# First group of four turned by TensorE, second feature block and output copies at its joint moved, third slot tile behind the gate sums

## The chip, the cores and the metric

One Trainium2 chip, one core of it. The metric is the time of the whole program on the device in microseconds, the median of several runs; a profile is one further execution.

## The reference, cut to what matters

Three parts follow each other on 2304 tokens of 512 features, all in float32.

```python
scores = q @ k^T / 8                       # 4 x 8 heads, 576 positions, 64 wide
x = (scores * gamma**(i-j), i >= j) @ v    # retention, then tokens x 512
logits = x @ w_gate + log1p(exp(x @ w_noise)) * noise
x = sum over the top 2 of 8 experts: w * (relu(x @ w1[e]) @ w2[e])
h = x @ w_in                               # 512 -> 2048
out = (h * clip(h + 3, 0, 6) / 6) @ w_out  # 2048 -> 512
```

## The kernel before, in words

The order of the work on each engine is the order in which the Python code emits it; nothing is rescheduled. Every engine (TensorE is PE, VectorE DVE, ScalarE ACT, GpSimd POOL, SyncE SP) takes its instructions in order, and a DMA issue stands in the order of the engine whose queue it uses. Buffers come from pools: a tile of a pool that is in use makes its first writer wait.

**Attention** runs over 18 token tiles of 128 (`attention`). After every third tile `gsum` and `gate` compute the logits of the gate for the group and append a generator `route`, which picks two experts a token and computes the slots of the token's rows in a DRAM tensor `xe`. Each `rstep()` advances the first generator by one `yield`; so `rstep()` calls, scattered over the program, set where routing stands between the other work. The matmuls at L332 to L335 count the tokens (ranks) from the picks `ra`. `send` scatters one row block into `xe` (L374), an indirect DMA of POOL.

**Experts** (`moe`) run in ten sweeps (`SW`), each over the slots of one expert or a part of them. A sweep reads its tokens from `xe`, turns them so that features lie on partitions, and does a first GEMM (L688, into `ga` or `gb`) and a second (L705) for 8 feature blocks; the second GEMM of a block is emitted by `flush` one block later. Expert 0's three tiles of 120 slots are turned by PE in the last turn of `attention` (`x_tile`, L655 to L658). Results go to a DRAM tensor `yd`.

**The last layer** (`moe2`) takes the tokens in groups `GR`: two tiles in `plain`, then four groups of four in `seven`. For each tile `x2_gather` fetches the two experts' rows of each token from `yd` (L830), `x2_mix` weights and adds them (L838 on ACT, L839 on DVE). Then the tile must be turned. DVE turns blocks of 32x32 only, so the mixed tile is written to `x2d` in DRAM (L859) and read back by four DMAs that place each block of 32 tokens (`x_blocks`, L633), after which one DVE transposition finishes it (L874). The first group of four is prepared while `plain` runs its 16 steps f, in `x2_prep(1, f - 1)`; the table `PLAN` says in which step s = f - 1 each tile is gathered, mixed, read back and turned. The reads of this group are issued on ACT's queue, those of later groups on POOL's.

`seven` computes the four products of a 2x2 block matrix with seven multiplications (`g1_seven`): sums of the weights lie ready in the DRAM tensor `wc`, and sums of the tokens are built by `x2_sums`; `x2_set` splits each of the seven token operands into a high and a low float32r part (L908, L909). A block p of the 8 has seven sets of six matmuls (L1072), whose intermediate sums ACT copies out of PSUM (`mc`, L1077), then the hidden layer of both halves c[0] and c[1] (`hidden`, L1103 to L1107), then by `flush` the second GEMM of the block before. The last `flush` of a group copies the finished output tiles out of PSUM (L1130) and writes them (L1132). `wc_load` loads the weights of a block; a tiny DMA `paced` that reads an ACT result (L981) holds SP's queue until the program has come that far.

```python
                self.ys[j] = self.x_blocks(rows, (self.nc.sync, self.nc.scalar, self.nc.gpsimd)[min(gi, 2)])
            ((0, 4, 6, 8), (0, 5, 7, 9), (1, 6, 8, 10), (4, 7, 9, 11)),
```

The second line is the group's row of `PLAN`: for each of its four tiles the step s of gather, mix, read back and turn.

Of the kernel before, what the change touches and what calls it, by code (L numbers as in the profile page):

```python
# [7 lines left out]
F32 = mybir.dt.float32  # L8
# [56 lines left out]
class K:  # L65
# [210 lines left out]
    def route(self, g0, G):  # L276
# [51 lines left out]
        yield  # L328
        o = 128 + g0 // 3 % 2 * 32
# [71 lines left out]
    def attention(self):  # L401
# [25 lines left out]
        for t in range(NT):  # L427
# [19 lines left out]
            if t + 1 == NT:  # L447
                xs = self.x_new(0)
                for j, tag in enumerate(("acc", "gb", "tp")):
                    self.x_tile(0, xs, j, tag)  # L450
# [20 lines left out]
        self.gsum(NT // 3 - 1)  # L471
        self.xt(NT - 1)
# [338 lines left out]
    def flush(self):  # L811
# [4 lines left out]
        if self.prev[-1][4]:  # L816
            self.fin[0](*self.fin[1:])
# [18 lines left out]
    def x2_mix(self, t, y):  # L836
        v = self.nc.vector
        self.nc.scalar.activation(y[0], y[0], AF.Copy, scale=self.gw[:, t, 0:1])  # L838
        v.scalar_tensor_tensor(y[0], y[1], self.gw[:, t, 1:2], y[0], op0=OP.mult, op1=OP.add)  # L839

    def x2_prep(self, gi, s):
# [11 lines left out]
        for j in range(G):  # L853
# [3 lines left out]
            if s == plan[j][1]:  # L857
                self.x2_mix(t0 + j, self.ys[j])
                self.nc.gpsimd.dma_start(rows, self.ys[j][0])  # L859
        for j in range(G):  # L860
            rows = self.x2d[(t0 + j) * P:(t0 + j + 1) * P]
            _, _, get, cut = plan[j]
            if s == get:
                self.ys[j] = self.x_blocks(rows, (self.nc.sync, self.nc.scalar, self.nc.gpsimd)[min(gi, 2)])
            if s == cut:
# [4 lines left out]
                else:  # L870
                    if j % 2 == 0:
                        self.raw2.append(self.big([P, 4, 2 * P]))
                    o = self.raw2[-1][:, :, c]
                    self.nc.vector.transpose(o.rearrange("p b (t j) -> p t b j", j=32),  # L874
                                             x.rearrange("p t (b i) -> p t b i", i=32))
        if gi and s == 10:
# [3 lines left out]
            self.x2_set(*((1, 2) if gi == 1 else (1,)))  # L880
        if gi and s == 12:
            self.x2_sums()
        if gi == 1 and s == 13:
            self.x2_set(5, 3)

    def x2_sums(self):
# [4 lines left out]
        t2, t3, t4 = (self.row([P, DM]) for _ in range(3))  # L891
        v.tensor_sub(t3, b22, b12)
        v.tensor_sub(b12, b12, b11)
        v.tensor_sub(t2, b22, b12)
        v.tensor_sub(t4, t2, b21)
        self.x2f.update({3: b22, 4: t4, 5: b12, 6: t2, 7: t3})

    PLAN = (((0, 2, 4, 5), (0, 2, 4, 5)),
            ((0, 4, 6, 8), (0, 5, 7, 9), (1, 6, 8, 10), (4, 7, 9, 11)),
# [12 lines left out]
    def pr_init(self):  # L912
# [4 lines left out]
        self.wcn, self.wcs, self.late = 0, {}, None  # L917
# [87 lines left out]
    def plain(self, t0, G):  # L1005

        for f in range(16):
# [7 lines left out]
            if fi == 0:  # L1015
                self.wc_load(p + 2 if p < 6 else p + 1, gh.bitcast(F32))
            if f == 15:
                self.x2_set(6, 4, 7)
# [8 lines left out]
    def seven(self, gi, t0, G):  # L1027

        X = self.x2s
        for p in range(8):  # L1030
# [7 lines left out]
            joint = p == 7 and gi + 1 < len(self.GR)  # L1038
# [3 lines left out]
            else:  # L1042
                h.append(self.hidden(c[1]))
            self.flush()
# [10 lines left out]
            if joint:  # L1055
# [6 lines left out]
    def g1_seven(self, X, W, begun):  # L1062
# [33 lines left out]
        v.tensor_add(h1[:, n:], a, c5)  # L1096
        return h0, h1
# [239 lines left out]
```

## Time and profile before

| | us |
|---|---|
| median of 3 runs | 966.65 (965.6 to 969.04) |
| the profiled execution | 966.33 |
| its span, first to last instruction | 964.5 |
| PE busy | 939.6 (97%) |
| DVE, ACT, POOL busy | 614.5, 471.5, 239.6 |
| mean granted clock | 0.993 |

PE is the engine that is nearly always busy. Its time falls into attention (to about 112 us), the ten expert sweeps (to about 563), `plain` (to about 616) and the four groups of `seven`. The end of a matmul is modelled and matmuls overlap, so from one start to the next is what a set costs.

### The profile page before, as it was taken

Reading aid. Unit: us, or ns where it says so; the run is one execution under the profiler, and the core shown is the slowest. Engines: PE = TensorE matmul, PEld = TensorE weight load, DVE = VectorE, ACT = ScalarE, POOL = GpSimd, SP = SyncE. Lnnn points to the kernel's source line nnn. Section 1 sums busy time; section 2 is a strip of 40 time slices with the busy share of each in tenths; the row PEclk is TensorE's granted clock in tenths of the full one; section 3 lists DMA queues with packets and bytes.
Section 4 is the critical chain, followed back from the end, with each engine's and each line's share of the span. In section 5 each row is a group of like instructions: output and inputs, shape, how many; then the busy total and the mean of one; then the engine's idle time right before and its main releaser. Section 6 shows DMA issues by size and latency. Waiting matters only on the chain.

```text
span 964.5 us, 17639 instructions
## 1 busy us (share of the span) xinstructions
PE 939.6 (97%) x6248; PEld 835.5 (87%) x6248; DVE 614.5 (64%) x1356; ACT 471.5 (49%) x1000; POOL 239.6 (25%) x327
## 2 busy tenths in 40 slices
PE   8999999999999999999999997899999999999997
PEld 6888788888898988888888886788899899989986
DVE  5688664877879888786866444645654564564342
ACT  4566533546555464646444443444454454445442
POOL 1245332322425242332410213015013211500000
PEclk9999999999999999999999999999999999999999
DMA  9783746886969889797627788558667756965551
GB/s 341 266 309 134 268 144 203 269 239 202 294 224 274 257 253 279 224 260 265 204 104 238 238 284 301 205 198 291 206 241 260 254 186 228 296 197 196 195 189 47
DMA packets 126271, 223.30 MB, mean 232 GB/s; under 512 B 13269, under 2 KB 63189, under 8 KB 126173
## 3 DMA queue, kind: packets, MB, share of 16 engines
q1 hardware_dynamic: 113757, 190.47, 59.8%
q0 software_dynamic: 9680, 29.77, 9.1%
q10 hardware_dynamic: 2736, 1.84, 0.6%
q8 instruction: 51, 0.84, 0.4%
q14 instruction: 47, 0.39, 0.1%
HBM read 165.01 MB, written 57.02 MB: 230 GB/s over the span
## 4 chain that ended last, share of the span: by engine, by line
PE 87%; DVE 4%; DMA 4%; issue 2%; ACT 2%; ACTq 0%; POOL 0%; SPq 0%; DVEq 0%
PE p L705 39%; PE ga L688 12%; PE gb L688 9%; PE mga L1072 7%; PE p L1072 5%; PE mtp L1072 2%; PE mgb L1072 2%; PE px L214 2%; PE sc L192 2%; PE p L175 2%; PE px L204 2%; DMA b<-wc 1%; DMA s<-x2d 1%; PE p L253 1%; PE p L238 1%
## 5 line engine op out<-in xcount | busy, mean ns | idle before, releaser
L705 PE MATMUL p<-b,h 128*120 128x512 f32 (+1 forms) x1056 | 262.7, 396 | 5.3 <-ACT h L1117 5.2
L705 PEld LDWEIGHTS p<-b,h 128*120 128x120 f32 (+1 forms) x1056 | 189.3, 185 | 48.3 <-ACT h L1117 6.0
L705 PE MATMUL p<-b,b 128*128 128x512 f32 x768 | 180.0, 390 | 0.0
L705 PEld LDWEIGHTS p<-b,b 128*128 128x128 f32 x768 | 142.2, 188 | 28.2
L688 PE MATMUL ga<-x,b 128*128 128x360 f32 (+1 forms) x768 | 134.0, 323 | 1.8 <-DVE h L747 1.8
L688 PEld LDWEIGHTS ga<-x,b 128*128 128x128 f32 x768 | 124.7, 188 | 10.8 <-DVE h L747 6.2
L591 POOL TENSOR_TENSOR cvl<-cvl,cvs 128x256 f32<-128x256 f32 x64 | 50.2, 784 | 228.3 <-ACT cva L572 167.9
L542 DVE TENSOR_TENSOR b<-b,b 128x512 fp32r<-128x512 f32 x128 | 90.1, 738 | 13.4 <-ACT b L541 12.9
L688 PE MATMUL gb<-b,b 128*128 128x256 f32 x672 | 90.0, 283 | 0.3 <-DVE b L644 0.3
L688 PEld LDWEIGHTS gb<-b,b 128*128 128x128 f32 x672 | 87.1, 190 | 1.5 <-DVE b L644 0.5
L830 POOL DMA_INDIRECT s<-yd,slotc x36 | 37.7, 1047 | 167.3 <-DVE x L909 50.9
L541 ACT ACTIVATE b<-b 128x512 fp32r<-128x512 f32 x128 | 74.0, 625 | 0.0
L1107 DVE SCALAR_TENSOR_TENSOR b<-s,b 128x512 fp32r<-128x512 f32 x64 | 44.3, 692 | 44.7 <-ACT b L1106 43.3
L1106 ACT ACTIVATE b<-s 128x512 fp32r<-128x512 f32 x64 | 40.5, 632 | 53.7 <-DVE s L1104 52.8
L592 POOL TENSOR_TENSOR cvl<-cvt,cvl 128x256 f32<-128x256 f32 x64 | 58.9, 920 | 5.0
L1103 ACT ACTIVATE s<-s,three 128x512 f32<-128x512 f32 x64 | 45.9, 717 | 26.2 <-DVE s L1093 26.2
L1072 PE MATMUL mga<-b,b 128*128 128x256 f32 x384 | 56.6, 283 | 2.1 <-DMA b<-wc 2.1
L1093 DVE TENSOR_TENSOR s<-p,mc 128x256 f32<-128x256 f32 x32 | 13.6, 424 | 69.2 <-PE p L1072 69.2
L1072 PEld LDWEIGHTS mga<-b,b 128*128 128x128 f32 x384 | 52.6, 191 | 5.0 <-DMA b<-wc 2.6
L747 DVE SCALAR_TENSOR_TENSOR h<-gb,h 128x256 fp32r<-128x256 f32 (+1 forms) x64 | 27.6, 432 | 44.6 <-PE p L705 33.6
L1077 ACT ACTIVATE mc<-mga 128x256 f32<-128x256 f32 x64 | 24.5, 383 | 55.7 <-PE mga L1072 54.3
L747 DVE SCALAR_TENSOR_TENSOR h<-ga,h 128x360 fp32r<-128x360 f32 (+1 forms) x64 | 32.6, 510 | 24.6 <-ACT h L746 24.6
(190 smaller groups left out, 1451.6 us busy)
## 6 DMA issues: line engine op xcount, KB each, us to landing
b<-wc SPq DMA_DIRECT2D x112, 512.0 KB
b<-in_moe_w_dram SPq DMA_DIRECT2D x64, 512.0 KB
wc<-b SPq DMA_DIRECT2D x32, 512.0 KB
s<-xe SPq DMA_DIRECT2D x140, 64.0 KB
s<-in_moe_w_in_dram SPq DMA_DIRECT2D x32, 256.0 KB
s<-in_moe_w_out_dram SPq DMA_DIRECT2D x32, 256.0 KB
b<-wc SPq DMA_DIRECT2D x32, 256.0 KB
yd<-s SPq DMA_DIRECT2D x24, 240.0 KB
```

What stands on the lines that cost most here:

```text
L541: self.nc.scalar.activation(h, a, AF.Copy)
L542: rest = lambda h=h, l=l, a=a: self.nc.vector.tensor_sub(l, a, h.bitcast(F32))
L591: nc.gpsimd.tensor_mul(lf, lf, s.bitcast(F32))
L592: nc.gpsimd.tensor_add(lf, t.bitcast(F32), lf)
L688: nc.tensor.matmul(p, a[k], b[:, k, :n], start=(i == 0), stop=(i == 11))
L705: nc.tensor.matmul(a[:R], x[:, c], y[:, fi, :], start=(first and i == 0), stop=(last and i == 2))
L747: nc.vector.scalar_tensor_tensor(hl, p, 0.0, hh.bitcast(F32), op0=OP.max, op1=OP.subtract)
L830: nc.gpsimd.indirect_dma_start(out=r, out_offset=None, in_=self.yd[0:rows], in_offset=bass.IndirectOffsetOnAxis(ap=self.slotc[:, t, k:k + ...
L1072: nc.tensor.matmul(t, w[:, u, k], x[:, z, k], start=(first and i == 0), stop=(last and i == 5), skip_group_check=True)
L1103: nc.scalar.activation(r, x, AF.Relu, bias=self.three)
L1106: nc.scalar.activation(h[:, 0], x, AF.Copy, scale=1.0 / 6.0)
L1107: v.scalar_tensor_tensor(h[:, 1], x, 1.0 / 6.0, h[:, 0].bitcast(F32), op0=OP.mult, op1=OP.subtract)
```

## The change

For the first group of four only (gi == 1) `x2_mix` writes its result in another order of columns, in four pieces, into a new row tile; `x2_pe` turns it with four PE products against the identity into a PSUM tile, and ACT copies that out. The writes to `x2d`, the reads and the DVE transpositions of this group are gone. The steps of `PLAN` move, and so do the sums and splits. In `plain` the first weights of the next group are loaded at f = 12 (`min(p + 2, 8)`) instead of f = 14, and operand 7 is split a step earlier. In the first block of `seven` the second half of the hidden layer is put off into the next block (`late`, as at the other joints), and the two output copies of `plain` to the end of the next block's seven products (`late_out`). In attention the last gate group's rank matmuls come one `yield` later, and the third slot tile of expert 0 is turned after the last `gsum`.

```diff
--- before.py
+++ after.py
@@ -326,6 +326,8 @@
         yield
         yield
         yield
+        if g0 + G == NT:
+            yield
         o = 128 + g0 // 3 % 2 * 32
         pr = self.pg[:, o:o + G * 8].rearrange("p (g e) -> p g e", g=G)
         for g in range(G):
@@ -446,8 +448,8 @@
             self.kv(t)
             if t + 1 == NT:
                 xs = self.x_new(0)
-                for j, tag in enumerate(("acc", "gb", "tp")):
-                    self.x_tile(0, xs, j, tag)
+                self.x_tile(0, xs, 0, "acc")
+                self.x_tile(0, xs, 1, "gb")
             self.rstep()
             if t + 3 < NT:
                 self.ks(t + 3)
@@ -469,6 +471,7 @@
             if t + 1 < NT:
                 self.wstep(WN)
         self.gsum(NT // 3 - 1)
+        self.x_tile(0, xs, 2, "tp")
         self.xt(NT - 1)
         self.gate(NT - 1, groups)
         self.rstep()
@@ -808,13 +811,16 @@
             for s in sw:
                 xs.pop(s)
 
-    def flush(self):
+    def flush(self, out=True):
         if self.prev is None:
             return
         for g in self.prev:
             self.g2(*g)
         if self.prev[-1][4]:
-            self.fin[0](*self.fin[1:])
+            if out:
+                self.fin[0](*self.fin[1:])
+            else:
+                self.late_out = self.fin
         self.prev = None
 
 
@@ -833,10 +839,18 @@
             y.append(r)
         return y
 
-    def x2_mix(self, t, y):
+    def x2_mix(self, t, y, turned):
         v = self.nc.vector
         self.nc.scalar.activation(y[0], y[0], AF.Copy, scale=self.gw[:, t, 0:1])
-        v.scalar_tensor_tensor(y[0], y[1], self.gw[:, t, 1:2], y[0], op0=OP.mult, op1=OP.add)
+        if not turned:
+            v.scalar_tensor_tensor(y[0], y[1], self.gw[:, t, 1:2], y[0], op0=OP.mult, op1=OP.add)
+            return y[0]
+        z = self.row([P, DM])
+        o = z.rearrange("t (b q i) -> t b q i", q=4, b=4)
+        b, a = (u.rearrange("t (q b i) -> t q b i", q=4, b=4) for u in y)
+        for q in range(4):
+            v.scalar_tensor_tensor(o[:, :, q], a[:, q], self.gw[:, t, 1:2], b[:, q], op0=OP.mult, op1=OP.add)
+        return z
 
     def x2_prep(self, gi, s):
 
@@ -855,13 +869,14 @@
             if s == plan[j][0]:
                 self.ys[j] = self.x2_gather(t0 + j)
             if s == plan[j][1]:
-                self.x2_mix(t0 + j, self.ys[j])
-                self.nc.gpsimd.dma_start(rows, self.ys[j][0])
+                self.ys[j] = self.x2_mix(t0 + j, self.ys[j], gi == 1)
+                if gi != 1:
+                    self.nc.gpsimd.dma_start(rows, self.ys[j])
         for j in range(G):
             rows = self.x2d[(t0 + j) * P:(t0 + j + 1) * P]
             _, _, get, cut = plan[j]
-            if s == get:
-                self.ys[j] = self.x_blocks(rows, (self.nc.sync, self.nc.scalar, self.nc.gpsimd)[min(gi, 2)])
+            if s == get and gi != 1:
+                self.ys[j] = self.x_blocks(rows, self.nc.gpsimd if gi else None)
             if s == cut:
                 x = self.ys.pop(j)
                 c = slice(j % 2 * P, (j % 2 + 1) * P)
@@ -871,32 +886,50 @@
                     if j % 2 == 0:
                         self.raw2.append(self.big([P, 4, 2 * P]))
                     o = self.raw2[-1][:, :, c]
+                    if gi == 1:
+                        self.x2_pe(x, o)
+                        continue
                     self.nc.vector.transpose(o.rearrange("p b (t j) -> p t b j", j=32),
                                              x.rearrange("p t (b i) -> p t b i", i=32))
-        if gi and s == 10:
+        if gi and s == (8 if gi == 1 else 10):
             self.x2s = {}
             r = self.raw2[0].rearrange("p (h k) n -> p h (k n)", h=2)
             self.x2f = {1: r[:, 0], 2: r[:, 1]}
-            self.x2_set(*((1, 2) if gi == 1 else (1,)))
-        if gi and s == 12:
-            self.x2_sums()
-        if gi == 1 and s == 13:
-            self.x2_set(5, 3)
-
-    def x2_sums(self):
+            self.x2_set(1)
+        if gi and s == (10 if gi == 1 else 12):
+            self.x2_sums(0)
+        if gi and s == (11 if gi == 1 else 12):
+            self.x2_sums(1)
+        if gi == 1 and s in self.FIRST:
+            self.x2_set(self.FIRST[s])
+
+    FIRST = {9: 2, 12: 5, 13: 3, 14: 7}
+
+    def x2_pe(self, x, o):
+
+        p = self.ps.tile([P, 4, P], F32, name="xp", tag="tp")
+        for b in range(4):
+            self.nc.tensor.transpose(p[:, b, :], x[:, b * P:(b + 1) * P], self.ident)
+        self.nc.scalar.activation(o, p, AF.Copy)
+
+    def x2_sums(self, part):
 
         v = self.nc.vector
         r0, r1 = (r.rearrange("p (h k) n -> p h (k n)", h=2) for r in self.raw2)
         b11, b21, b12, b22 = r0[:, 0], r0[:, 1], r1[:, 0], r1[:, 1]
-        t2, t3, t4 = (self.row([P, DM]) for _ in range(3))
-        v.tensor_sub(t3, b22, b12)
-        v.tensor_sub(b12, b12, b11)
+        if part == 0:
+            t3 = self.row([P, DM])
+            v.tensor_sub(t3, b22, b12)
+            v.tensor_sub(b12, b12, b11)
+            self.x2f.update({3: b22, 5: b12, 7: t3})
+            return
+        t2, t4 = (self.row([P, DM]) for _ in range(2))
         v.tensor_sub(t2, b22, b12)
         v.tensor_sub(t4, t2, b21)
-        self.x2f.update({3: b22, 4: t4, 5: b12, 6: t2, 7: t3})
+        self.x2f.update({4: t4, 6: t2})
 
     PLAN = (((0, 2, 4, 5), (0, 2, 4, 5)),
-            ((0, 4, 6, 8), (0, 5, 7, 9), (1, 6, 8, 10), (4, 7, 9, 11)),
+            ((0, 5, 0, 6), (0, 6, 0, 7), (1, 7, 0, 8), (3, 8, 0, 9)),
             ((0, 3, 4, 7), (1, 4, 5, 8), (3, 6, 7, 10), (4, 7, 8, 11)))
 
     def x2_set(self, *names):
@@ -914,7 +947,7 @@
         self.wc = self.dr.tile([8, 4, P, 1024], F32, name="wc")
         self.pa = {}
         self.pq = [j for p in range(8) for j in self.pr_jobs(p)]
-        self.wcn, self.wcs, self.late = 0, {}, None
+        self.wcn, self.wcs, self.late, self.late_out = 0, {}, None, None
         self.paced = self.dr.tile([1, 1], F32, name="paced")
 
     def pr_jobs(self, p):
@@ -1013,9 +1046,9 @@
             self.wstep(0, 32 + p)
             gh, gl = self.glu(self.wcs[p][fi], self.x2, G * P, "ga" if fi == 0 else "gb")
             if fi == 0:
-                self.wc_load(p + 2 if p < 6 else p + 1, gh.bitcast(F32))
+                self.wc_load(min(p + 2, 8), gh.bitcast(F32))
             if f == 15:
-                self.x2_set(6, 4, 7)
+                self.x2_set(6, 4)
             self.wstep()
             self.flush()
             if self.acc is None:
@@ -1035,13 +1068,13 @@
                 self.wc_load(gi * 8 + p + 1, c1)
 
             c = self.g1_seven(X, self.wcs.pop(gi * 8 + p), begun)
-            joint = p == 7 and gi + 1 < len(self.GR)
+            joint, start = p == 7 and gi + 1 < len(self.GR), gi == 1 and p == 0
             h = [self.hidden(c[0])]
             if joint:
                 self.x2_set(2, 5, 6, 4, 3, 7)
-            else:
+            elif not start:
                 h.append(self.hidden(c[1]))
-            self.flush()
+            self.flush(not start)
             if self.acc is None:
                 self.acc = [self.pacc([P, DM]) for _ in range(G)]
             new = []
@@ -1052,7 +1085,7 @@
 
             for fi, x in enumerate(h):
                 entry(x, fi)
-            if joint:
+            if joint or start:
                 self.late = lambda x=c[1], entry=entry: entry(self.hidden(x), 1)
             self.prev = new
             self.fin = (self.o_out, t0, self.acc)
@@ -1094,6 +1127,9 @@
         mul(a, 7, False, True)
         v.tensor_sub(h1[:, 0:n], a, c4)
         v.tensor_add(h1[:, n:], a, c5)
+        if self.late_out:
+            self.late_out[0](*self.late_out[1:])
+            self.late_out = None
         return h0, h1
 
     def hidden(self, x):
```

ACT at the joint, steps f = 8 to 11 of `plain`, before (s_ are row tiles, h_ the hidden layer, s_7365 the mixed tile 2):

```order
L838 ACTIVATE s_7365<-s_7365,gw 128x512
L633 DMA s_7538<-x2d 32x4x128 x4
L1115 ACTIVATE h_7558<-ga,three 128x256
L1117 ACTIVATE h_7543<-h_7558 128x256
L838 ACTIVATE s_7465<-s_7465,gw 128x512
L633 DMA s_7577<-x2d 32x4x128 x4
L1115 ACTIVATE h_7597<-gb,three 128x256
L1117 ACTIVATE h_7582<-h_7597 128x256
L633 DMA s_7610<-x2d 32x4x128 x4
L1115 ACTIVATE h_7630<-ga,three 128x256
L1117 ACTIVATE h_7615<-h_7630 128x256
L633 DMA s_7647<-x2d 32x4x128 x4
```

and with the change, steps f = 7 to 10 (b_7541 and b_7623 hold the turned pairs of tiles):

```order
L844 ACTIVATE s_7330<-s_7330,gw 128x512
L913 ACTIVATE b_7541<-xp 128x4x128
L1151 ACTIVATE h_7563<-ga,three 128x256
L1153 ACTIVATE h_7548<-h_7563 128x256
L844 ACTIVATE s_7365<-s_7365,gw 128x512
L913 ACTIVATE b_7541<-xp 128x4x128
L1151 ACTIVATE h_7606<-gb,three 128x256
L1153 ACTIVATE h_7591<-h_7606 128x256
L844 ACTIVATE s_7434<-s_7434,gw 128x512
L913 ACTIVATE b_7623<-xp 128x4x128
L941 ACTIVATE b_7630<-b_7541 128x512
L1151 ACTIVATE h_7648<-ga,three 128x256
```

Each run of four reads of `x2d` has gone from between mix and relu; in its place stands one copy out of PSUM, and the split of the first operand (L941) comes in step f = 9.

ACT at the first block of `seven` and the start of the next, before (p_7298 and p_7299 are the output tiles of `plain`, mga the first PSUM tile of the seven products):

```order
L1103 ACTIVATE s_7891<-s_7827,three 128x512
L1106 ACTIVATE b_7894<-s_7827 128x512
L1103 ACTIVATE s_7897<-s_7828,three 128x512
L1106 ACTIVATE b_7900<-s_7828 128x512
L1130 ACTIVATE s_7909<-p_7298 128x512
L1130 ACTIVATE s_7912<-p_7299 128x512
L1077 ACTIVATE mc<-mga 128x256
L1077 ACTIVATE mc<-p_7926 128x256
L1077 ACTIVATE mc<-mga 128x256
L1077 ACTIVATE mc<-mtp 128x256
```

and with the change:

```order
L1139 ACTIVATE s_7903<-s_7839,three 128x512
L1142 ACTIVATE b_7906<-s_7839 128x512
L1110 ACTIVATE mc<-mga 128x256
L1139 ACTIVATE s_7937<-s_7840,three 128x512
L1142 ACTIVATE b_7940<-s_7840 128x512
L1110 ACTIVATE mc<-p_7926 128x256
L1110 ACTIVATE mc<-mga 128x256
L1110 ACTIVATE mc<-mtp 128x256
L1166 ACTIVATE s_7998<-p_7298 128x512
L1166 ACTIVATE s_8001<-p_7299 128x512
```

The first copy of the next block (mc from mga) now stands behind one half of the hidden layer; the second half follows it, and the output copies come after that block's last copy.

PE in the first expert sweep, at the ranks of the last gate group, before (p_245 holds the gate's sums, h_ and p_1799 to p_1801 are the second GEMM's input and output):

```order
L705 MATMUL p_1801<-b_1093,h_1774 120x512
L688 MATMUL ga<-x_1711,b_1491 128x360 x4
L688 MATMUL ga<-x_1711,b_1492 128x360 x4
L688 MATMUL ga<-x_1712,b_1491 128x360 x4
L332 LDWEIGHTS ones
L332 MATMUL p_245<-macc,ones 128x8
L335 LDWEIGHTS tri
L335 MATMUL p_245<-ra,tri 128x8
```

and with the change:

```order
L691 MATMUL ga<-x_1712,b_1491 128x360 x4
L708 MATMUL p_1799<-b_1093,h_1821 120x512
L708 MATMUL p_1799<-b_1094,h_1821 120x512
L708 MATMUL p_1799<-b_1093,h_1822 120x512
L708 MATMUL p_1800<-b_1093,h_1821 120x512
L708 MATMUL p_1800<-b_1094,h_1821 120x512
L708 MATMUL p_1800<-b_1093,h_1822 120x512
L708 MATMUL p_1801<-b_1093,h_1821 120x512
L708 MATMUL p_1801<-b_1094,h_1821 120x512
L708 MATMUL p_1801<-b_1093,h_1822 120x512
L334 LDWEIGHTS ones
L334 MATMUL p_245<-macc,ones 128x8
```

The nine matmuls of the second GEMM have moved from behind the rank matmuls to ahead of them.

## Rows read from the trace of the kernel before

**Rows 1.** Busy time by stretch of 20 us around the joint, granted clock in column PEclk.
```profile
580.00:600.00 20.00, 15.02 (x83) 12.77 (x82) 9.37 (x18) 6.86 (x14) 6.79 (x8) 0.91 0.86 294
600.00:620.00 20.00, 17.64 (x105) 15.66 (x104) 12.75 (x25) 8.44 (x19) 1.92 (x2) 0.92 0.54 186
620.00:640.00 20.00, 18.13 (x124) 16.71 (x123) 8.40 (x16) 9.54 (x20) 0.94 (x1) 1.00 0.68 237
640.00:660.00 20.00, 20.00 (x126) 18.09 (x125) 10.41 (x19) 9.53 (x18) 8.69 (x13) 1.00 0.75 271
```

**Rows 2.** Timeline of PE at the joint: start us, us, operation [idle before <-releaser].
```profile
580.54 1.59 PE L688 MATMUL gb<-x,b 128*128 128x256 f32 x12
...
583.36 1.60 PE L688 MATMUL ga<-x,b 128*128 128x256 f32 x12
...
590.60 1.66 PE L705 MATMUL p<-b,h 128*128 128x512 f32 x6 [2.49 <-ACT h L1117]
...
596.13 2.88 PE L705 MATMUL p<-b,h 128*128 128x512 f32 x6 [2.44 <-ACT h L1117]
...
616.10 1.18 PE L1072 MATMUL mga<-b,b 128*128 128x256 f32 x6 [2.14 <-DMA b<-wc]
...
628.30 0.98 PE L1072 MATMUL mga<-x,b 128*128 128x256 f32 x6 [1.87 <-ACT mc L1077]
...
631.27 5.63 PE L705 MATMUL p<-b,b 128*128 128x512 f32 x24
...
647.24 0.88 PE L1072 MATMUL mga<-b,b 128*128 128x256 f32 x6
...
652.27 2.91 PE L705 MATMUL p<-b,b 128*128 128x512 f32 x12
```

**Rows 3.** Timeline of ACT at the joint; ACTq are its DMA issues.
```profile
582.66 0.72 ACT L838 ACTIVATE s<-s,gw 128x512 f32<-128x512 f32 x1 [0.73 <-DMA s<-yd,slotc]
...
586.82 2.31 ACTq L633 DMA_DIRECT2D s<-x2d  x4
...
589.17 0.47 ACT L1115 ACTIVATE h<-ga,three 128x256 f32<-128x256 f32 x1 [3.09 <-issue]
...
626.91 1.06 ACT L1130 ACTIVATE s<-p 128x512 f32<-128x512 f32 x2
```

**Rows 4.** Chain of work that ended last, at the joint: start us, us, what.
```profile
581.45 5.34 DMA x2d<-s
...
587.21 4.84 DMA s<-x2d
```

**Rows 5.** PE turning blocks of 128x128: two pieces of its timeline, and line L253.
```profile
105.79 0.66 PE L253 MATMUL p<-cst,x 128*128 128x128 f32 x4
...
106.28 0.17 PE L332 MATMUL p<-macc,ones 128*128 128x8 bf16 x1
...
L253 PE MATMUL p<-cst,x x72: 272/273/332, 15.2 to 111.2; 128*128 128x128 f32 x72
```

**Rows 6.** DVE groups by form, 560 to 625 us: xcount | busy us, mean ns.
```profile
L1118 DVE SCALAR_TENSOR_TENSOR h<-h,h 128x256 fp32r<-128x256 f32 x16 | 6.8, 425 | 7.7 <-ACT h L1117 6.3 <-issue 1.0 <-PE p L705 0.5
...
L839 DVE SCALAR_TENSOR_TENSOR s<-s,gw,s 128x512 f32<-128x512 f32 x4 | 3.0, 751 | 1.7 <-DMA s<-yd,slotc 0.8 <-ACT h L1115 0.7 <-ACT s L838 0.2
```

**Rows 7.** The load of the first weights for p = 1 (SP), and a slow load (chain).
```profile
618.05 1.27 SPq L975 DMA_DIRECT2D b<-wc  x3
...
650.66 10.21 DMA b<-wc
```

**Rows 8.** Timeline of PE at the hand-over to the experts, and at sweep 2.
```profile
111.97 0.81 PE L272 MATMUL p<-cst,pl 128*128 128x16 f32 x6 [0.54 <-DVE pos L354]
...
122.28 0.17 PE L335 MATMUL p<-ra,tri 128*128 128x8 bf16 x1 [1.37 <-DVE ra L325]
...
170.57 2.25 PE L688 MATMUL ga<-x,b 128*128 128x360 f32 x12 [0.53 <-DVE h L747]
```

**Rows 9.** Chain before the last of these waits.
```profile
158.41 2.06 DMA s<-xe
```

## The prediction

> **What bounds the kernel now.** I read the busy time by stretches first, then PE's own timeline where PE is not full, and only then the engine that PE waited for there. TensorE (PE) is busy for the whole of 640 to 660 us, and 5.0, 2.4 and 1.9 us short of it in the three stretches from 580 to 640 [rows 1]. The granted clock is 0.91 and 0.92 in the first two of these: part of each ran at 1.2 instead of 2.4 GHz. So the place to win is the joint, where the two plain token tiles end and the first group of four begins.
>
> PE's timeline names the waits [rows 2]: 2.49 and 2.44 us for ACT's h, 2.14 us for weights from wc, 1.87 us for ACT's mc. ACT is not busy then. Its row before the first wait is a run of DMA issues of 2.31 us (reading x2d), and the relu that PE needs stands behind it with 3.09 us idle [rows 3]. The issues stand because x2d must have been written: the chain has 5.34 us for a write and 4.84 us for a read back [rows 4]. ACT works in order, so a DMA that waits there holds the hidden layer of the running tiles.
>
> **The price of the joint.** From the first product of step f = 8 (583.36) to the second GEMM of p = 1 (631.27) takes 47.91 us [rows 2]. Undisturbed it would be eight steps of 2.82 us (580.54 to 583.36), two sets of seven products of 5.03 us each (647.24 to 652.27), and half a step, 1.40 us, for the second GEMM of f = 15: 22.56 + 10.06 + 1.40 = 34.0 us. **The excess is 13.9 us**, idle time (8.9 us in the four waits shown), what ran at half the clock (the six products at 596.13 take 2.88 us, those at 590.60 1.66), and short fillings of the pipeline around each wait.
>
> **What the change does to it, part by part.**
>
> 1. *The trip through DRAM goes.* Four writes to x2d from POOL's queue, sixteen reads from ACT's queue and four DVE transposes leave; the ACT stall and the late tiles go with them. That returns the 13.9 us, if the new way is on time.
>
> 2. *PE turns instead.* 16 products of 128x128 against the identity. The same operation at L253 comes four in 0.49 us (105.79 to 106.28), 0.12 us each; one lasts 0.273 us by its record [rows 5]. They lie on PE, which is the bound, so all of it counts: 16 x 0.12 = 2.0 us; from above, with no overlap, 16 x 0.273 = 4.4 us. I take 2.0, since the rows in question are the same instruction back to back.
> The Trainium skill ("TensorE: Matmul & The Clock Gate", Part 4: PE-mode transpose) gives about 275 ns for one in a kernel and says that a copy out of PSUM must follow. As an estimate from its figure the 16 would cost 4.4 us and the sum below would be 9.4 instead of 11.8; the trace shows the 275 ns as the length of one, but not as its share when four follow each other.
>
> 3. *The mix in four pieces.* DVE now writes each mixed tile as four 128x128 pieces, already in the order that PE turns. 128x512 takes 0.751 us and 128x256 0.425 [rows 6]; the line through these puts 128x128 at 0.26 us, its upper bound is the 0.425. A tile so costs 1.0 to 1.7 us in place of 0.75 for the mix and about 0.7 for the turn. It must be done when PE has finished the second GEMM of the step before. For the first tile: ACT's mix stands where that of tile 1 stood (582.66, 0.72 us long) [rows 3]; without that one's wait of 0.73 and the DVE mix of the step before it (0.75) it ends at about 581.9. DVE needs 1.0 to 1.7 more, PE gets there at 583.36 [rows 2]: on time, or 0.2 late. The three later tiles have a step each. ACT gets a copy out of PSUM of some 0.55 us (two of that size take 1.06 [rows 3]) in steps 7 to 10; with relu (0.47), the copy to h, the mix (0.72) and a first split that is about 2.8 us of work in a step that grows from 2.82 to 3.3. It fits, and ACT is no longer held by DMA issues.
>
> 4. *The gathers.* The mix of tile 1 had 0.73 us to wait for its rows on ACT [rows 3]. Each mix now comes one step (2.8 us) later and the last gather is issued a step earlier, without x2d writes between. I expect no wait.
>
> 5. *First weights of the group of four.* They are loaded at f = 12 instead of f = 14, which covers the 2.14 us [rows 2]; their buffers are those of steps already done.
>
> 6. *First block of the sevens.* Before, ACT did both hidden halves and the two output copies (1.06 us [rows 3]) before the copy mc that PE waited 1.87 us for. Now mc comes after one half, then the second half, then the copies of the next products, then the output copies, which release two accumulators. By the durations in these rows the copy of the third product comes some 0.4 us late for the sixth; the output copies end while PE is still in the first accumulators. Queued behind on SP are the two output writes, which nobody waits for. I take 0.4 us.
>
> 7. *Weights for p = 1.* They are asked for at the first mc of p = 0, as before. Before, the issue was at 618.05 [rows 7] and PE needed them some 6 us later (three sets of 0.72 before 628.30, less its wait of 1.87 [rows 2]). Now mc stands behind three splits on ACT, some 2.4 us after the first product, and p = 1 begins 5.03 + 1.40 us after it: 4.0 us after the issue, and the weights that come last are needed 2.8 us later still. One load took 10.21 us [rows 7]. Bounds of this wait: 0 and 10.2 - 6.8 = 3.4 us. No gather is tied to that moment, so I take 0.3.
>
> 8. *The early part.* The rank products of the last gate group go behind a second GEMM, which removes the 1.37 us for ra; the third slot tile goes behind the gate sums, which removes up to 0.54 us for the logits [rows 8]. Of the first I expect little to stay: at 170.57 PE already waits 0.53 us at the end of a row of DVE and ACT work that started when a read of xe landed (158.41 + 2.06) [rows 8, 9]. That read follows the scatter of the slots, and DVE computes the slots in the same place of its order as before. PE that arrives 1.4 us sooner waits 1.4 us longer there, unless the scatter moves too. The 0.54 moves the logits and so the scatter. I take 0.6; bounds 0 and 1.9.
>
> **Sum.** 13.9 - 2.0 - 0.4 - 0.3 + 0.6 = 11.8 us. The profiled execution took 966.33 us (span 964.5), so 954.5; the median of the runs shown is 0.3 us higher, so the forecast for the median is **954.8 us**. From 640 us on PE is full and its loads are paced by its own progress, so I let the gain reach the end.
>
> **Rivals.**
>
> - *The early gain stays whole* (the scatter is not what rows 8 end on): 1.3 us more, 953.5. For: the read of xe is only one link; against: no PE entry lies between it and the wait. Chance 0.12.
> - *The weights for p = 1 become the wait*: 3.4 instead of 0.3 us, 957.9. For: the 10.21 us [rows 7], and the copy mc moves little while PE moves much; against: no gather is tied to that moment. Chance 0.12.
> - *The turns don't overlap*: each of the 16 takes its full 0.273 us because one follows another kind of product, 2.4 us more, 957.2. This is also the skill's figure above. Against: the four in 0.49 us [rows 5]. Chance 0.06.
> - *The joint stays bound by memory*, so that the change doesn't do what it says: the gathers land as late as the slow load, ACT stands at the mix of the last tile as it did at x2d. Its rows are asked for at about 584 and needed at 590; landing after 10.2 us [rows 7] costs some 4.3 us and one spell of slow clock (0.09 of 20 us [rows 1], 1.7 us): 960.8. If it happens on two tiles, 966.8, no change. For: DVE and ACT both waited for gathers [rows 3]. Against: those waits were under 0.8 us and the trips that shared the engines go. Chance 0.07, 0.03 of it for two tiles.
> - *DVE's pieces make it slower.* The pieces write runs of 32 elements at strides; if a piece costs much more than its size says, PE waits for z at every turn. A step has 3.3 us and DVE's other work in it takes 1.6 (two of 0.425, one of at most 0.75 [rows 6]), so the wait starts at t = 0.43 us a piece; four tiles lose 16t - 6.8 us, and the clock drops as before, 0.17 of 20 us or 3.4 us [rows 1]. At the price of a whole row (0.75) that is 8.6 us, 963.4; at 1.2 us a piece 15.8 us, **970.6, slower than before**. For it speaks only that no row shows this form; against it the near proportional price in rows 6. Chance 0.03, 0.02 for the slower end.
>
> **How the numbers follow.** The forecast itself has 0.60. Its own bounds (terms 2, 6, 7 and 8) and the first three rivals run from 952.4 to 958.8; the last two, 0.10, are left out, with some room for terms that I have at nothing. A measurement of this kernel can tell about 0.3%, 2.9 us, from no change. All cases but 0.06 lie below 963.7: faster 0.94; the two-tile case and prices of a piece between 0.75 and 1.1 us give 0.04 for the same; 0.02 slower.
>
> **What would show it.** Right: between 580 and 640 us PE shows no wait over 1 us and the granted clock is 1.00 in all three stretches; ACT has no DMA issue there; the turns take about 0.5 us per four; the first of the sevens starts some 8 us earlier; the 1.37 us at the ranks is gone and the wait at 170 has grown to about 1.5 us. Wrong: a wait of PE at the turns for DVE's pieces, a wait for wc at the second block of sevens, an ACT row with a gather as releaser, or no wait at all at 170.

## The result, and the profile after

The changed kernel takes 955.8 us (median of 4 runs, 955.3 to 957.51), the kernel before 967.63 beside it: 11.8 us less; the ratio on record, with its 95% interval, is 0.9882 [0.9859, 0.9906]. The forecast was 954.8 (952.4 to 958.8). The profiled execution of the changed kernel took 957.51 us (span 955.7), the slowest of the four.

The stretches of 20 us around the joint of the changed kernel, for [rows 1]; the columns are stretch, length, PE's busy time (instructions), its granted clock, DMA share, GB/s:

```profile
580.00:600.00 20.00, 18.30 (x119) 1.00 0.72 259
600.00:620.00 20.00, 19.39 (x137) 1.00 0.64 235
620.00:640.00 20.00, 20.00 (x126) 1.00 0.57 202
```

PE is short of full by 1.7 and 0.6 us, where it was short by 5.0, 2.4 and 1.9, and its granted clock stays at 1.00. PE's timeline there, for [rows 2]:

```profile
582.60 0.65 PE L912 MATMUL xp<-cst,s 128*128 128x128 f32 x4 [0.26 <-issue]
583.01 1.68 PE L691 MATMUL ga<-x,b 128*128 128x256 f32 x12
585.39 1.67 PE L708 MATMUL p<-b,h 128*128 128x512 f32 x6 [0.70 <-ACT h L1153]
587.80 0.63 PE L912 MATMUL xp<-cst,s 128*128 128x128 f32 x4 [0.74 <-DVE s L852]
...
608.88 0.87 PE L1105 MATMUL mga<-b,b 128*128 128x256 f32 x6
...
617.46 0.88 PE L1105 MATMUL mga<-x,b 128*128 128x256 f32 x6
618.95 0.98 PE L1105 MATMUL mtp<-x,b 128*128 128x256 f32 x6 [0.61 <-DMA b<-wc]
...
621.21 5.63 PE L708 MATMUL p<-b,b 128*128 128x512 f32 x24
```

The waits of over 2 us for ACT's h, the one for wc at the first of the sevens (now 608.88) and the one for mc (now 617.46) are gone. New are three small ones at the first two turns, 1.70 us together (0.26, 0.70 and 0.74), and 0.61 for wc at p = 1, the second block of the sevens. The two early waits of [rows 8] are gone as well; the one near 170 us is unchanged, 0.54 for 0.53:

```profile
112.57 0.81 PE L272 MATMUL p<-cst,pl 128*128 128x16 f32 x6
...
123.47 0.17 PE L337 MATMUL p<-ra,tri 128*128 128x8 bf16 x1
...
169.34 2.25 PE L691 MATMUL ga<-x,b 128*128 128x360 f32 x12 [0.54 <-DVE h L750]
```

To see where the time went I divided PE's timeline at six starts that all kernels have. The last two columns are a second profile of each kernel, on other chips (before_again and after_again below). In us:

| from one start on PE to the next | before | after | forecast | before again | after again |
|---|---|---|---|---|---|
| L253's four ahead of the first ranks (105.79; after 106.96) to the first product of expert 0 (112.63; 113.23) | 6.84 | 6.27 | -0.5 | 8.25 | 7.61 |
| to the product near 170 us | 57.94 | 56.11 | -0.1 | 57.50 | 56.37 |
| to the first of the sevens | 445.53 | 439.54 | | 445.83 | 437.09 |
| to the second GEMM of p = 1 | 15.17 | 12.33 | -11.2 (both) | 15.19 | 12.23 |
| to the last second GEMM (947.03; 938.17) | 315.76 | 316.96 | 0 | 316.10 | 317.73 |
| all | 841.24 | 831.21 | -11.8 | 842.87 | 831.03 |

So in the first pair the joint (third and fourth row) gave 8.8 us instead of 11.2, the early part (first two) 2.4 instead of 0.6, and 1.2 were given back in the last row, where I had expected nothing. In the second pair it was 11.7, 1.8 and 1.6. The forecast's total came out nearly right in both (10.0 and 11.8), with errors of both signs in it. The spans of the first pair differ by 8.8 us only: the changed kernel is 1.2 us late at the first of these starts already.

### The profile page after: what moved, and what is told of

It is laid out like the page before. It is cut to its first block, busy times and chain, and to the rows that moved or that the text cites. A ratio compares the mean times of both kernels' runs of the same rounds, so it can differ in the third digit from the quotient of the medians.

```text
span 955.7 us, 17648 instructions
## 1 busy us (share of the span) xinstructions
PE 938.4 (98%) x6264; PEld 834.8 (87%) x6264; DVE 613.6 (64%) x1364; ACT 473.1 (50%) x1004; POOL 235.9 (25%) x323
## 4 chain that ended last, share of the span: by engine, by line
PE 89%; DMA 4%; DVE 3%; ACT 1%; issue 1%; POOL 1%; SPq 1%; DVEq 0%; ACTq 0%
PE p L708 40%; PE ga L691 13%; PE gb L691 10%; PE mga L1105 6%; PE p L1105 4%; DMA b<-wc 3%; PE mtp L1105 2%; PE mgb L1105 2%; PE px L214 2%; PE sc L192 2%; PE p L175 2%; PE px L204 2%; PE p L253 1%; PE p L238 1%; PE p L112 1%
## 5 line engine op out<-in xcount | busy, mean ns | idle before, releaser
L545 DVE TENSOR_TENSOR b<-b,b 128x512 fp32r<-128x512 f32 x128 | 90.2, 740 | 13.4 <-ACT b L544 13.2
L749 ACT ACTIVATE h<-gb 128x256 fp32r<-128x256 f32 (+1 forms) x64 | 25.1, 393 | 46.1 <-PE gb L691 37.8
```

The source lines that it names most:

```text
L545: rest = lambda h=h, l=l, a=a: self.nc.vector.tensor_sub(l, a, h.bitcast(F32))
```

## The experiments

**The joint again.** Both kernels once more, with no edit.

> The kernel before, once more, for a second profile of its joint beside the others. From the product behind the wait near 170 us to the second GEMM of p = 1 the first profile took 460.7 us; the eight profiles with the change that had no stall at the turns took 449.2 to 450.4. If the excess of 13.9 us at the joint belongs to the order of the work, this one has the waits for h, for wc and for mc again and some 460 us there; if it belonged to that one execution or chip, 455 or less.

> The changed kernel once more, as the base for the runs beside it. What stands in its order must come again: PE's wait of 0.70 us for ACT's h after step f = 8 and of 0.74 for DVE's pieces at the second turn. If the waits of PE for wc after 640 us (0.65 and 0.7) come from that one execution's transfers, they move or vanish here, and the time is 1 us less; if they come from the order, they stand at the same two places.

The kernel before took 963.95 us in one run. From the product near 170 us to the second GEMM of p = 1, the stretch that ends with the joint, it needs 461.0 us (460.7 at first), so the excess is not an accident of one execution. PE's waits between 555 and 950 us in this profile (total, times, longest):

```profile
PE p L705 <- ACT h L1117: 5.5, 4, 3.5
PE mga L1072 <- DMA b<-wc: 2.1, 1, 2.1
PE mga L1072 <- ACT mc L1077: 1.9, 1, 1.9
PE mtp L1072 <- DMA b<-wc: 0.4, 1, 0.4
```

The waits for wc and mc come again to 0.03 us (2.11 and 1.87); those for h vary between the steps and hardly in their sum. The changed kernel again: 951.43 us beside 964.93, 13.5 us less, ratio 0.9856 [0.983, 0.9881]. Its turns:

```profile
576.50 1.54 PE L708 MATMUL p<-b,h 128*128 128x512 f32 x6
577.88 0.60 PE L912 MATMUL xp<-cst,s 128*128 128x128 f32 x4
578.24 1.67 PE L691 MATMUL ga<-x,b 128*128 128x256 f32 x12
579.75 1.56 PE L708 MATMUL p<-b,h 128*128 128x512 f32 x6
581.14 0.60 PE L912 MATMUL xp<-cst,s 128*128 128x128 f32 x4
```

No wait: the expectation that 0.70 and 0.74 come from the order fell. Of the twelve profiles with the change only the first has PE wait for ACT's h at the joint. No run undid the trip through x2d alone; that its end removed these waits is read from these profiles. A step with a turn takes 3.26 us (577.88 to 581.14), one without 2.82 [rows 2], so four turned blocks cost 0.44 us and the 16 of them 1.8. The waits for wc after 640 us did come again, at p = 4 of the second and third group of four.

**Terms 5 and 6, undone one at a time.**

```diff
-                self.wc_load(min(p + 2, 8), gh.bitcast(F32))
+                self.wc_load(p + 2 if p < 6 else p + 1, gh.bitcast(F32))
```

> The changed kernel with the first weights of the group of four asked for at f = 14 again. By term 5 PE waits 2.14 us for wc ahead of the first of the sevens, and the time is 2.1 us more. Rival: with the trips through x2d gone the load has the engines for itself, comes in time for the later start all the same or nearly so, and the wait is under 0.7 us.

```diff
-            joint, start = p == 7 and gi + 1 < len(self.GR), gi == 1 and p == 0
+            joint, start = p == 7 and gi + 1 < len(self.GR), False
```

> The changed kernel with the second hidden half and the output copies of the plain tiles back in front of the first copy mc of the group of four. By term 6 PE waits 1.5 to 1.9 us for mc, and the time is 1.5 us more or a little above (the wait for wc at p = 1 may hide behind it). Rival: the second half and the copies fit, since ACT has no transfers to issue any more: under 0.5 us.

wc14: 953.78 us beside 964.7, ratio 0.9881 [0.9866, 0.9896]; no_late_out: 953.35, 0.988 [0.9858, 0.9901]; both some 2.4 us above after_again's 0.9856, though the intervals overlap. The profiles are clearer. The first fence is PE in wc14, with the clock in two of its stretches (columns as above); the second is no_late_out.

```profile
605.48 1.59 PE L1105 MATMUL mga<-b,b 128*128 128x256 f32 x6 [3.04 <-DMA b<-wc]
606.87 1.48 PE L1105 MATMUL mgb<-x,b 128*128 128x256 f32 x6
608.15 1.26 PE L1105 MATMUL p<-x,b 128*128 128x256 f32 x6
609.25 0.88 PE L1105 MATMUL mga<-x,b 128*128 128x256 f32 x6
...
607.00:609.00 2.00, 2.00 (x11) 0.50 0.53 147
609.00:611.00 2.00, 2.00 (x18) 1.00 0.92 320
```

```profile
613.21 1.12 PE L1105 MATMUL mga<-x,b 128*128 128x256 f32 x6 [1.89 <-ACT mc L1110]
614.13 1.49 PE L1105 MATMUL mtp<-x,b 128*128 128x256 f32 x6
...
614.00:616.00 2.00, 2.00 (x11) 0.50 0.98 245
```

Each undone part brings its wait back, 3.04 us where 2.14 was forecast and 1.89 where 1.87, and both rivals fall. The wait isn't its whole price: after it PE runs at half the clock for a while, and in wc14 three sets of six products take 3.77 us (605.48 to 609.25), 1.6 more than three times 0.72. From the product near 170 us to the second GEMM of p = 1 wc14 takes 453.5 us and no_late_out 452.4, against 449.3 to 450.4 in the eight undisturbed profiles with the change, own_gh to held_twice_own and after_again: some 3.6 and 2.6 us more.

**The early part, term 8.**

```diff
-        if g0 + G == NT:
-            yield
```

> The changed kernel with the rank products of the last gate group back ahead of the second GEMM. PE waits some 1.4 us for ra again. Theory K (kept): what the move saved there reaches the end, so the time is 1.2 to 1.5 us more than with it, about 957.2, and the wait of PE near 170 us stays at 0.5. Theory G (given back, as term 8 of the prediction has it): the first tokens of the next expert come no sooner by the move, so the wait near 170 us shrinks from 0.54 to 0 when PE arrives later, and the time grows by 0.8 us at most, from the measured 955.8 to 956.6 or less.

```diff
                 self.x_tile(0, xs, 1, "gb")
+                self.x_tile(0, xs, 2, "tp")
...
-        self.x_tile(0, xs, 2, "tp")
         self.xt(NT - 1)
```

> The changed kernel with the third slot tile back ahead of the gate sums. The wait of 0.5 us of the logits for pos returns. Theory K: it reaches the end, 0.5 us more, about 956.3. Theory G: the slots and the scatter move with it, so here too 0.5 us more. A rival that the move did nothing: no wait, the same time.

Both edits together:

> The changed kernel with both early moves undone (rank products and third slot tile back), so the joint's changes alone. In the two executions compared first, the way from the first product of the first expert to the one behind the wait near 170 us shrank by 1.83 us, while no_yield against after_again on one chip shrank by 0.27 only. Theory K (the whole early gain stays): 1.9 us slower than the changed kernel (1.4 for ra and 0.5 for pos), and the waits for ra and pos of before are back. Theory G (the 1.37 is given back at 170): 0.6 to 1.1 us slower, what the slot tile alone is worth; and in the profile the reads of xe come as long after the first expert's first product as in after_again, about 42.4 us.

no_yield and no_slot ran beside after_again: 953.21 us (0.9873 [0.985, 0.9896]) and 952.49 (0.9872 [0.9848, 0.9896]), 1.8 and 1.1 us above its median, with intervals that overlap. no_early: 954.2 beside 965.95, 0.9883 [0.9862, 0.9904], 2.5 and 3.1 above held_twice and held_twice_own, which do the early part as the changed kernel does and ran beside it; each of its five runs (953.13 or more) lies above all eight of theirs (952.74 or less). The first two rows of the table sum to 63.98 us in after_again, 64.07 in no_yield, 64.82 in no_slot and 66.12 in no_early: undone alone, the rank products cost 0.1 us and the slot tile 0.8; undone together, 2.1. Nine profiles that leave this part as the changed kernel has it spread from 62.4 to 64.8, though, so these sums price neither move alone. The 1.8 us of no_yield needn't stem from here either: in its profile PE waits 1.46 us for wc at p = 1, 0.51 in after_again. In no_slot the wait for pos is 0.16 us, not the 0.5 expected. In no_yield the wait for ra is 1.31 us, but the one near 170 is gone, as theory G has it; in no_early both are there, as K has it:

```profile
118.61 0.17 PE L335 MATMUL p<-ra,tri 128*128 128x8 bf16 x1 [1.31 <-DVE ra L325]
...
165.65 2.25 PE L689 MATMUL ga<-x,b 128*128 128x360 f32 x12
```

```profile
120.33 0.17 PE L335 MATMUL p<-ra,tri 128*128 128x8 bf16 x1 [1.25 <-DVE ra L325]
...
168.29 2.25 PE L689 MATMUL ga<-x,b 128*128 128x360 f32 x12 [0.54 <-DVE h L748]
```

What the wait near 170 hangs on is read from the chain of work that ended last (start us, us, what), here of the changed kernel:

```profile
136.24 2.00 PE ga L691 x12
...
138.63 0.64 ACT b L544
...
139.90 0.18 DVE b L545
...
141.45 0.95 POOL xe L1203
...
149.01 5.92 DMA xe<-s,free
154.98 0.34 SPq L636
```

The reads of xe follow the last of seven fills by POOL; these stand behind DVE, which stands behind ACT's split of a weight, which stands behind the relu of a product of PE. In no_early the same chain runs from PE's product at 135.17 to the one at 168.29, 33.12 us; here from 136.24 to 169.34, 33.10. **The chain starts on PE**, so a PE that is earlier moves it along. In the first profile of the kernel before it starts on PE too, at another place; in the second at this one (134.28 to 167.41, 33.13). The first:

```profile
155.28 1.43 PE ga L688 x12
...
156.78 1.12 SPq L633
```

Whether the rank products alone cost next to nothing to undo, and why, isn't settled: in no_yield the fills start 3.7 us behind that product (133.44, 137.11), in the changed kernel 5.2, in no_early 4.5.

**The stall at the first turns.** In the first profile of the changed kernel ACT's relu of f = 7 stood for 2.59 us, and PE's waits of 0.70 and 0.74 came from it:

```profile
580.66 0.71 ACT L844 ACTIVATE s<-s,gw 128x512 f32<-128x512 f32 x1
583.96 0.47 ACT L1151 ACTIVATE h<-gb,three 128x256 f32<-128x256 f32 x1 [2.59 <-PE xp L912]
```

By the program's order this relu waits for its product, which ended at 580.95, and for one DMA: the pacing read of f = 4, which reads 4 bytes of a buffer of the hidden pool that the relu writes next.

```
L1151 ACTIVATE h_7522<-gb,three 128x256 [waits DMAHW3_49,PE_49]
```

The turn that the row names isn't among these. I tried to take the DMA's hold away, and to lengthen it:

```diff
+    OWN = ("cvt", "cva", "cvt", "cva", "cvt", "cva", "cvt", "cvs")
...
-            gh, gl = self.glu(self.wcs[p][fi], self.x2, G * P, "ga" if fi == 0 else "gb")
+            own = None if fi else self.sb.tile([P, G * P], F32R, name="gh", tag=self.OWN[p], bufs=1 + (p < 7))
+            gh, gl = self.glu(self.wcs[p][fi], self.x2, G * P, "ga" if fi == 0 else "gb", own)
...
-        gh, gl = self.hid([P, n]), self.hid([P, n])
+        gh, gl = own or self.hid([P, n]), self.hid([P, n])
```

> The changed kernel, with a buffer of its own for the first hidden half of the even steps of the plain tiles (the half that the pacing read of 4 bytes reads). Theory S (slot): ACT's relu of f = 7, idle 2.59 us until 583.96, waited for the pacing read of f = 4 to land (issued at 573.94, 10.0 us earlier), since it writes the buffer that this read holds. Then the relu now starts at once behind the mix, some 2.5 us earlier, PE's two waits of 0.70 and 0.74 go, and the time falls by 1.4 us, to about 954.4. Rival E (engines): ACT and DVE have too much work in the steps with a turn, and the relu stood behind the turn itself, as the row names it. Then both waits stay and the time stays at 955.8.

```diff
+        self.held = self.dr.tile([1, 1], F32, name="held")
...
                 self.wc_load(min(p + 2, 8), gh.bitcast(F32))
+                self.nc.sync.dma_start(self.held, gh.bitcast(F32)[0:1, 0:1])
```

> The changed kernel with a second read of 4 bytes of the same hidden half, issued behind the two weight loads of its step, so that the buffer is held longer. Theory S (slot): whoever writes that buffer next waits until this read lands; behind 1 MB, at the 290 GB/s of these stretches, it lands 3.5 us later than the first one. ACT's relu or copy to h three steps later stalls, PE waits for h between f = 3 and f = 13 in several steps, 1 us or more each, and the time grows by 3 to 10 us. Rival E: the buffers are not what the relu waited for in the first profile: nothing changes but two tiny transfers, under 0.5 us.

> As held_twice, but the half that is read has a buffer of its own (the edit of own_gh). Theory S: nobody needs that buffer soon, so the stalls of held_twice are gone and the time is that of the changed kernel within 0.5 us. Rival: if held_twice is slower for the transfers themselves (the SP queue, the order of the loads), this one is as slow.

own_gh: 951.8 us, ratio 0.9857 [0.983, 0.9883], the same as after_again. That decides nothing, since after_again had no stall to remove. held_twice 951.71 (0.9852 [0.9827, 0.9877]), held_twice_own 951.1 (0.9856 [0.9829, 0.9882]): no stall in either, so theory S fails as a cost of every execution. Even a read behind two loads of 512 KB landed before the buffer's next writer needed it. What is left is that the pacing read landed late once, 10.0 us after its issue: it follows from the two waits by elimination, but no run showed it again.

The stall isn't why the first profile of the changed kernel is 5.3 us longer than the second (spans 955.7 and 950.4). They differ by 5.8 us ahead of the first start of the table already (106.96, 101.13), before any row of PE that the change moves, and from there to the last second GEMM they take 831.21 and 831.03. In both profiles of the first pair PE waits there as follows, and in no other profile; here the changed kernel:

```profile
100.18 1.16 PE L204 MATMUL px<-b,s 128*128 128x128 f32 x8 [0.87 <-ACT s L242]
102.26 0.43 PE L214 MATMUL px<-b,b 128*64 128x128 f32 x2 [0.92 <-DVE b L194]
```

What causes these waits is open. The intervals of the two ratios, 0.9882 and 0.9856, overlap, so their difference needs no cause.

**The waits given back.** From p = 1 to the end the changed kernel takes 316.1 to 317.8 us in the ten profiles that leave this part alone, the kernel before 315.8 and 316.1. The difference is PE's waits for wc at p = 4 of the second and third group of four, 0.48 to 1.96 us in all: without such waits the stretch takes 315.6 to 316.0 us in each of the ten and in both profiles of the kernel before. The first of them in the changed kernel, and the transfers ahead of it (columns as above):

```profile
735.49 0.97 PE L1105 MATMUL mtp<-x,b 128*128 128x256 f32 x6 [0.65 <-DMA b<-wc]
...
726.34:729.56 3.22, 3.22 (x17) 1.00 1.03 368
729.56:733.16 3.60, 3.60 (x23) 1.00 1.04 396
```

The DMA engines are busy all the time there. The Trainium skill ("DMA: Bandwidth & Descriptors", section "Where 436 GB/s comes from") gives 435 GB/s as the ceiling of the ports to SBUF, and about 358 GB/s of HBM as what binds transfers between HBM and SBUF. The 396 of this row lie below the first figure and above the second, which does not bind here. Two attempts to take bytes out of this stretch, in the last tile's row of `PLAN`, the second with the weights of p = 1 earlier as well:

```diff
-            ((0, 3, 4, 7), (1, 4, 5, 8), (3, 6, 7, 10), (4, 7, 8, 11)))
+            ((0, 3, 4, 7), (1, 4, 5, 8), (3, 6, 7, 10), (5, 7, 8, 11)))
```

> The changed kernel with the gather of the last tile of each later group of four one half step later (5 instead of 4). In the profiles of all five kernels with the change but no_slot, PE waits 0.65 to 1.5 us for wc at p = 4 of the second and third group of four, in a stretch in which the transfers are at 0.96 to 1.04 of their share: eight gathers, two writes of x2d, its reads and 1.8 MB of weights. Theory B (bytes): the loads come late because these share the engines; two gathers fewer in that stretch take 0.5 MB out, 1.3 us at 390 GB/s, the two waits go, and the time falls by up to 2 us. Rival: the wait is the weights' own buffer or order; then it stays, and the time too.

```diff
-            ((0, 3, 4, 7), (1, 4, 5, 8), (3, 6, 7, 10), (4, 7, 8, 11)))
+            ((0, 3, 4, 7), (1, 4, 5, 8), (3, 6, 7, 10), (6, 8, 9, 12)))
...
-                self.wc_load(min(p + 2, 8), gh.bitcast(F32))
+                self.wc_load(p + 2, gh.bitcast(F32))
```

> The changed kernel with two edits against its waits for wc: the weights of p = 1 of the first group of four asked for at f = 14, not at the first copy mc; and in the later groups the last tile gathered two half steps later (6, mixed at 8, read at 9, cut at 12). Theory B (bytes): the waits of 0.5 to 1.5 us at p = 1 and of 0.7 to 1.4 us at p = 4 of two groups go, 2 to 3 us less than the changed kernel, ratio about 0.983. Rival: the early load stands on SP for its buffers and takes them from the copies of the joint, so that PE waits there instead; then no gain at the joint, and 1 to 2 us from p = 4 alone.

plan2: 950.47 beside 965.95, ratio 0.9846 [0.9824, 0.9868]. It has no wait in the second group of four, and in the third still 0.65 us. But six of the ten profiles that leave this part alone have none in the second group either (own_gh, which the expectation counts otherwise, is one), so plan2 shows nothing. spread: 950.91 beside 964.7, 0.9855 [0.984, 0.987]. Its wait at p = 1 is gone (11.60 us from the first of the sevens to the second GEMM of p = 1, instead of 12.2 to 13.2), and so is the one in the third group, which all ten have (0.43 to 1.27 us). But it pays later, 317.2 us to the end, 0.42 of it in a wait for wc at p = 4 of the first group of four, where the changed kernel has none, and 0.49 in one for mc. Neither can be told from the changed kernel by its time.

That bytes cause these waits is not shown. The kernel before has stretches with DMA engines as busy, and PE full:

```profile
746.00:749.00 3.00, 3.00 (x21) 1.00 1.03 382
749.00:752.00 3.00, 3.00 (x15) 1.00 1.05 318
```

## Why the prediction came out as it did

It was right in its result and in the mechanism of the joint. That it came within 1.0 us of the median is in part luck: two terms were wrong and, with a stall that I had no term for, cancelled in part. In after_again the gain was 13.5 us and the ratio of 0.9856 near the favourable end of the range (952.4 of 966.65 is 0.9853). The ends of the range aren't worked out: terms 6 to 8 at their best give 952.8, and the worst of the first three rivals 957.9.

- *Terms 1 to 3, right.* With the trips through x2d gone, PE in the first profile has no wait over 1 us between 580 and 640, ACT issues no DMA there, and the clock is 1.00 in all three stretches. The joint gave 11.7 us in the undisturbed pair, 11.2 were forecast. In the first pair it gave 8.8; the waits at the turns in that execution are 1.70 us of what is missing. The turns cost 1.8 us (2.0 forecast). The pieces of the mix take 1.14 us a tile (1.0 to 1.7 forecast), and the first turn was 0.26 us late in one profile, on time in the other. The Trainium skill's figure ("TensorE: Matmul & The Clock Gate", Part 4, about 275 ns a block) is not the price here: by it a step with a turn would take 1.1 us more, and it takes 0.44. The rivals on turns, on DVE's pieces and on memory fall.
- *Term 4, right.* No mix of this group waits for a gather.
- *Term 5, right, its price too low.* Undone, it costs 3.04 us of waiting, not 2.14, and the half clock behind it.
- *Term 6, right.* The 1.87 us are gone, and mc has no wait where I had kept 0.4.
- *Term 7, undersized.* The weights for p = 1 come 0.51 to 1.46 us late, in nine of the twelve profiles, not 0.3. That is the rival's mechanism at a fraction of its 3.4.
- *Term 8, wrong.* The step that failed: "Of the first I expect little to stay", because the chain to the wait at 170 started with a read of xe that "follows the scatter of the slots". The rows just ahead of that read show SP released by a product of PE at 155.28. I had stopped one link short. The wait didn't grow to 1.5 but stayed at 0.54, and 1.8 to 2.4 us stayed instead of 0.6 (2.5 to 3.1 by the runs of no_early), as in the rival *the early gain stays whole*. This is shown for both moves together only.
- *"From 640 us on PE is full ..., so I let the gain reach the end", wrong by 1.2 to 1.6 us.* PE was full in the rows of before, and in places the transfers were too, which I had not looked at. What was lost are waits for wc; what makes these loads late stays open.

## What to carry to other kernels

Follow a chain of waits back until it reaches the engine that bounds the kernel: if it starts there, it moves along with work saved ahead of it, and the gain need not be lost at its end. Test it by undoing the parts singly and together, and against the spread of profiles with no edit there. Look at the transfers of every stretch that a gain has to pass through, not at the busy engine alone. And see what follows a wait of the bounding engine: in wc14 3 us of idling cost 1.6 us more at half the clock.

## What the hardware showed that I had not expected

- After a wait of 3.04 us (wc14) the granted clock is 0.50 between 607 and 609 us and 1.00 between 609 and 611, after one of 1.89 us (no_late_out) it is 0.50 between 614 and 616; waits of 0.5 to 0.7 us leave it at 1.00 in the same stretch of the changed kernel. 0.50 is 1.2 GHz. The wait's length alone doesn't decide: in the kernel before, PE's 1.87 us for mc, which end at 628.30, leave the clock at 1.00.

```profile
626.00:628.00 2.00, 0.43 (x4) 1.00 0.52 137
628.00:630.00 2.00, 1.70 (x14) 1.00 0.85 281
```

- Four blocks of 128x128 turned back to back between two other GEMMs take 0.36 us from their start to the next product (577.88 to 578.24) and lengthen the step by 0.44, though one lasts 0.272 us by its record (0.273 at L253 [rows 5]).
- One relu is made by the program to wait for a read of 4 bytes that only paces a queue, since it writes the buffer that is read. That this read caused the stall of 2.59 us is inferred from the relu's two waits; it came in one profile of twelve.
